# Attention, a mixture of experts and a feed-forward block in one kernel: activations carried across pairs, conversions moved, operands awaited singly, the plain block first

## The chip, the cores and the metric

One core of a Trainium2 chip runs the whole program. The metric is device time in microseconds (us): three runs of the kernel before gave a median of 2175.69 us (2173.25 to 2175.99). Engines are named as in the profile: PE does matrix products (PEld its weight loads), DVE and POOL elementwise work, ACT activations and copies, SP issues DMAs.

## The reference

Everything is float32. `q`, `k`, `v` have shape (4, 8, 576, 64).

```
x = attention(q, k, v)            # heads 0-3: a local window of 32; heads 4-7: every 32nd position, causal
x = x.transpose(0, 2, 1, 3).reshape(2304, 512)
P = exp(x @ w_gate - max)         # 2304 x 8
8 times: P /= row sums; P /= column sums; P *= 2304 / 8
for e in range(8): out += P[:, e] * (relu(x @ w1[e]) @ w2[e])     # w1[e] 512 x 1024, w2[e] 1024 x 512
h = out @ w_in                    # w_in 512 x 2048, stored as float64
g = where(h > 0, h, exp(min(h, 0)) - 1)
return g @ w_out                  # w_out 2048 x 512, stored as float64
```

## The kernel before

**Numbers.** PE multiplies in the format fp32r. Every operand is held as a rounded high part and a low part that carries the rest (`splits`, `low`: a cast on ACT, then a subtraction on DVE or POOL), and each product is three matmuls: high by high, high by low, low by high.

**Tiles.** The 2304 tokens go in two phases: phase 0 does 1024, phase 1 does 1024 and a plain block of 256. A hidden dimension is worked in *pairs* of two blocks of 128 columns: pairs 0 to 31 are the eight experts (four each, "MoE"), pairs 32 to 39 the last feed-forward block ("MoE2"). `gemm1` is the first product of a pair for 1024 tokens in Strassen's way (Winograd's form): seven products of six matmuls (128x512) each instead of eight. Its operands are seven sums of the tokens, B11, B21, B22, T1 to T4, held in `xb`, and seven sums of the weights. Three PSUM banks s1, s2, s3 gather the products; DVE adds between them (`add`, L943), so that the second use of s2 (S3 by T3) has to wait until `u2 = s2 + a1` has read it. `act` starts the activation of a finished quarter: a generator `activate` whose steps (ACT, DVE, and for MoE2 ACT and DVE again) `advance` takes one at a time. At the end of `gemm1` all are drained (L988). `gemm1_plain` is the ordinary first product for the 256 tokens. `gemm2` is the second product: for pairs taken two at a time (a *group*), two halves of four token tiles, 96 matmuls in all, in four banks `ybank`, which `finish` adds into `acc`.

**Order.** The order of every engine's queue is written out by hand: an engine runs its instructions in the order in which the program emits them. The program emits PE's matmuls and calls `gap` after every three of them in a first product (L938) and every three in a second product (L1030). `gap` puts one step each of side work into the queues: `prep_step` (the split of the next weights), `build_step` (the making of `xb` for the next layer: `build_a`, `build_b`, `build_plain`), `gate_step` (the gate's logits), and the generators in `gens`, each at its rate: the rest of the attention, `sinkhorn` (eight rounds of row and column sums), and `weigh` followed by `conversions` (float64 weights to float32, 32 jobs of seven DVE instructions and a store; the tile `val` has one buffer, so the next job begins when the store has landed). A generator's fourth entry says whether it runs in second products only: true for `sinkhorn` (rate 0.4), false for the conversions (rate 0.54). Builds run in second products only.

`ready(key)` emits all that is left of a named build: before a first product `a` (B11, B21), before its second product all of `b`. In phase 1 a group runs gemm1, plain, gemm1, plain, second product, plain second product.

The lines that matter are these:

```
if banks or alone_now[0] is None:          # gap, L755: builds
    for _ in range(BUILD_RATE): build_step()
...
ready((ph, moe2, "b"))                     # gemm1, L962
s2 = bank(); whole(prod(s2, S2, T2))
u2 = tmp("u2"); add(u2, s2, a1)
...
while acts: advance(acts)                  # gemm1, L988
```

Of the kernel before, what the change touches and what calls it, by code (L numbers as in the profile page):

```python
# [23 lines left out]
P = 128  # L24
# [16 lines left out]
HT = HALF // P  # L41
PW = 256
# [28 lines left out]
def sparse_attention_moe_kernel(ctx: ExitStack, tc: tile.TileContext, a, out):  # L71
# [159 lines left out]
    def build_a(src):  # L231

        hi, lo = xb
        todo = [(hi[:, x, c], lo[:, x, c], src(c + c0), ve if c else po_) for x, c0 in ((B11, 0), (B21, 2)) for c in (0, 1)]
        yield from splits(todo)

    def build_b(a, b):

        hi, lo = xb

        def minus(x, y, out=None):
            if out is None:
                out = hp_.tile([P, HALF], F32, tag="hh" if len(made) % 2 else "hl", name="t")
                made.append(out)
            ve.tensor_tensor(out=out, in0=x, in1=y, op=ALU.subtract)  # L245
            return out

        made = []
        t1 = [minus(b(c), a(c)) for c in (0, 1)]
        yield True  # L250
        t2 = [minus(b(c + 2), t1[c]) for c in (0, 1)]
        yield True

        def both(x, t, engs):
            for c in (0, 1):
                se.copy(hi[:, x, c], t[c])  # L256
            yield True
            for c in (0, 1):
                low(hi[:, x, c], lo[:, x, c], t[c], engs[c])
            yield True  # L260
# [236 lines left out]
    def att_s4(u):  # L497
# [144 lines left out]
    def build_step():  # L642
        if builds and next(builds[0][1], 0) == 0:
            builds.pop(0)

    def ready(key):
        while any(x[0] == key for x in builds):
            build_step()

# [84 lines left out]
    def after_attention():  # L734
# [5 lines left out]
        late["xp"] = [ffn.tile([P, 3, 2, PW], F32R, name=f"xp{hl}") for hl in "hl"]  # L740
        late["g"] = ctx.enter_context(tc.tile_pool(name="g", bufs=3))
        late["h"] = ctx.enter_context(tc.tile_pool(name="hplain", bufs=4))
# [3 lines left out]
        late["sink"] = sinkhorn()  # L746
        gens.append([late["sink"], SINK_RATE, 0.0, True])

    gens = []

    def gap(banks):
# [24 lines left out]
    def sinkhorn():  # L776
# [3 lines left out]
        yield True  # L780
        p1 = bank()
# [3 lines left out]
        p2 = bank()  # L785
        pe.matmul(p2[:, 0:1], ones[:1, :], small[:1, 1:2], start=True, stop=True)
# [7 lines left out]
        for it in range(8):  # L794
# [5 lines left out]
            yield True  # L800
            pc = bank()
            pe.matmul(pc[:, :E], ones, part, start=True, stop=True)
# [119 lines left out]

    def gemm1(ph, p, early=None):


        n = prep_state["now"] = ph * PAIRS + p
        w = slot_of(n, "done1")[:2]
        moe2 = p >= MOE1_PAIRS
        last = len(PHASES[ph]) == 1
        acts, hs = [], {}  # L930

        def prod(dst, wi, xi, start=True):
            for c in products(dst, w, xb, wi, xi, start=start):
                if c == 1 and last:
                    used(n, 1)
                yield c

        def whole(gen):  # L938
            for _ in gen:
                gap(False)  # L940

# [9 lines left out]

        ready((ph, moe2, "a"))
        s1 = bank()
        whole(prod(s1, A11, B11))
        a1 = tmp("a1")
        se.copy(a1, s1)  # L956
        if early:
            early()
            whole(prod(s1, A12, B21, start=False))
            act(s1, 0, 0)  # L960
# [8 lines left out]
        whole(prod(s3, S1, T1))  # L969
        advance(acts)  # L970
        whole(prod(s2, S3, T3, start=False))
        u3, c22 = tmp("u3"), tmp("c22")
        add(u3, s2, a1)
        add(c22, s3, u3)
        act(c22, 1, 1)
        advance(acts)
        if not early:
            whole(prod(s1, A12, B21, start=False))
            act(s1, 0, 0)
            advance(acts)  # L980
        whole(prod(s2, A22, T4, start=False))
        add(s2, s2, a1)
        act(s2, 1, 0)
        advance(acts)
        whole(prod(s3, S4, B22, start=False))
        add(s3, s3, u2)
        act(s3, 0, 1)
        while acts:  # L988
            advance(acts)
        return hs  # L990

    def gemm1_plain(ph, p):
        n = ph * PAIRS + p
        w = slot_of(n, "done1")[:2]
        ready((ph, p >= MOE1_PAIRS, "plain"))
        hs, acts = [], []
        for w1, w2, x2 in ((A11, A12, 1), (S1, A22, 2)):
            m = bank()
            for wi, xi in ((w1, 0), (w2, x2)):
                for _ in products(m[:, :PW], w, late["xp"], wi, xi, start=xi == 0, stop=xi != 0):  # L1000
                    gap(False)
            g = late["g"].tile([P, HALF], F32, tag="g", name="g")[:, :PW] if p >= MOE1_PAIRS else None
            hs.append([late["h"].tile([P, PW], F32R, tag=t, name=t) for t in ("ph", "pl")] + [g])
            acts.append(activate(p, m[:, :PW], PW, hs[-1]))
            advance(acts)
        while acts:
            advance(acts)
        used(n, 7)
        return hs

    def gemm2(ph, pairs, parts, tiles, t0):


        n0 = ph * PAIRS
        base = PHASES[ph][0][0]
        sums = [ybank() for _ in range(tiles)] if len(pairs) > 1 else [None] * tiles
        for p, hs in zip(pairs, parts):
            _, _, w2h, w2l = slot_of(n0 + p, "done")
            first, last = p == pairs[0], p == pairs[-1]
            for tt in range(tiles):  # L1020
                y = sums[tt] = sums[tt] or ybank()
                cs = slice(tt * P, (tt + 1) * P)
                for f in range(2):
# [6 lines left out]
                    gap(True)  # L1030

# [49 lines left out]

    def x1_a(ph):
        late["xa"] = r = raw("rawa")
# [6 lines left out]

    def x1_b(ph):
        r = late["xa"]
# [3 lines left out]

    def x1_plain(ph):
        r = late["p"].tile([P, KD, PW], F32, tag="rawp", name="rawp")
        for c in range(KD):
            pt = transposed(ybank(), 2 * HT, PW // P, c)  # L1100
            yield True
# [29 lines left out]
    def whole2(ph, pairs, hs):  # L1131
        for half in range(2):
            gemm2(ph, pairs, [by_half(x, half) for x in hs], HT, PHASES[ph][0][0] + half * HALF)
            if pairs[-1] == MOE1_PAIRS - 1:
                start_build((ph, True, "ab"[half]), (x1_a, x1_b)[half](ph))
        if len(PHASES[ph]) == 1:
            free_w2(len(pairs))


    h_prev = None  # L1140
    for p in range(SOLO):
        h_now = gemm1(0, p, early=(lambda: None) if p == 0 else None)
        if p:
            whole2(0, [p - 1], [h_prev])
        h_prev = h_now
    finish_gen(rest)


    for ph, blocks in enumerate(PHASES):
        for p in range(0 if ph else SOLO, PAIRS, GROUP):  # L1150
# [6 lines left out]
            for x in pairs:  # L1157
                hs.append(gemm1(ph, x, early=(lambda: None) if x == MOE1_PAIRS else None))
                if h_prev:
                    whole2(0, [SOLO - 1], [h_prev])  # L1160
                    h_prev = None
                if len(blocks) > 1:
                    hp.append(gemm1_plain(ph, x))
            if ph == 0 and p == PAIRS - GROUP:
                x_loads()
                start_build((1, False, "a"), build_a(lambda c: late["xa"][:, c]))
                start_build((1, False, "b"), x_b())
                start_build((1, False, "plain"), x_plain())
            whole2(ph, pairs, hs)
            if len(blocks) > 1:  # L1170
                gemm2(ph, pairs, hp, PW // P, blocks[1][0])
                free_w2(GROUP)
                if pairs[-1] == MOE1_PAIRS - 1:
                    start_build((ph, True, "plain"), x1_plain(ph))
            if ph == 0 and pairs[-1] == 2 * PER_E - 1:
                late["weigh"] = weigh()
                gens.append([late["weigh"], CONV_RATE, 0.0, False])

# [6 lines left out]
GATE_WAIT = 2  # L1185
GATE_WAIT1 = 2
RE_AT, RE_IN = 2, (4, 6)
# [3 lines left out]
X_DELAY = 4  # L1191
SINK_RATE = 0.4
CONV_RATE = 0.54

# [21 lines left out]
```

## Time and profile before

| | |
|---|---|
| median of three runs | 2175.69 us |
| the profiled execution | 2175.51 us |
| its span, first to last instruction | 2173.7 us, 26993 instructions |
| mean granted PE clock | 0.976 of full speed |
| busy share of the span | PE 95%, PEld 78%, DVE 61%, ACT 34%, POOL 29% |
| the chain that ended last | PE 62%, DVE 5%, ACT 3% |

A matmul's shown duration (0.39 us) is longer than the distance to the next one, because they are pipelined; so a busy PE need not be at its peak, and a stretch is better judged by how many matmuls it holds. "Idle" stands ahead of the arrow to what ended it. The chain and the waits name the last releaser only.

### The profile page before, as it was taken

What the parts mean: (1) busy time and instruction counts of PE and PEld (TensorE: products, weight loads), DVE (VectorE), ACT (ScalarE), POOL (GpSimd) and SP (SyncE); (2) the same over time, 40 slices, a digit from 0 to 9 for tenths busy, and PEclk for the clock granted to TensorE, in tenths of its full rate; (3) what the DMA queues carried; (4) which work ended last, traced back from release to release, by engine and by line L of the source; (5) the groups of instructions that cost most, each with busy time, mean ns of one, the idle gap of its engine ahead of it and who ended that gap; (6) DMA issues with size and microseconds to landing.
All of it is one profiled execution on the core that took longest, in us unless ns stands there. A gap on an engine that the chain in (4) does not pass through costs nothing.

```text
span 2173.7 us, 26993 instructions
## 1 busy us (share of the span) xinstructions
PE 2062.8 (95%) x10196; PEld 1697.5 (78%) x10196; DVE 1331.7 (61%) x2163; ACT 746.1 (34%) x1705; POOL 626.7 (29%) x709
## 2 busy tenths in 40 slices
PE   9889899999988999899999999999999999988999
PEld 7767677777766888677778888888888888867887
DVE  5676756888777855666664444444554445555555
ACT  6655322222222223355432222222222222234443
POOL 2332322333222333333342222222222222222220
PEclk8889999999999999899999999999999999999999
DMA  9632112333333311111321111111111111110111
GB/s 180 131 86 61 56 39 78 99 119 117 117 120 99 97 39 58 39 49 42 105 68 40 39 39 39 39 49 40 40 48 39 39 43 45 39 29 21 40 31 56
DMA packets 141171, 138.94 MB, mean 64 GB/s; under 512 B 67168, under 2 KB 105968, under 8 KB 141040
## 3 DMA queue, kind: packets, MB, share of 16 engines
q1 hardware_dynamic: 140080, 137.00, 21.7%
q8 instruction: 80, 1.31, 0.3%
q14 instruction: 51, 0.42, 0.1%
q10 hardware_dynamic: 960, 0.21, 0.1%
HBM read 121.46 MB, written 18.09 MB: 64 GB/s over the span
## 4 chain that ended last, share of the span: by engine, by line
PE 62%; DVE 5%; ACT 3%; DMA 1%; issue 1%; POOL 0%; SPq 0%; DVEq 0%; ACTq 0%
PE ybank L1026 34%; PE bank L881 28%; ACT g L904 1%; ACT g L903 1%; DVE xl L153 1%; DVE u L943 1%; DMA w_conv<-val 1%; DVE t L245 1%; ACT hh L908 1%; DVE g L906 0%; DMA w2raw<-in_moe_w 0%; DVE bank L943 0%; DVE c L943 0%; DVE acc L1040 0%; ACT xh L256 0%
## 5 line engine op out<-in xcount | busy, mean ns | idle before, releaser
L881 PE MATMUL bank<-xh,w1h 128*128 128x512 f32 x1120 | 454.9, 406 | 71.3 <-DVE u L943 42.8
L1026 PE MATMUL ybank<-w2h,hh 128*128 128x512 f32 x1280 | 505.5, 395 | 6.1 <-DVE kT L421 2.2
L1026 PE MATMUL ybank<-w2h,hl 128*128 128x512 f32 x1280 | 499.9, 391 | 0.0
L1026 PE MATMUL ybank<-w2l,hh 128*128 128x512 f32 x1280 | 499.8, 390 | 0.0
L881 PE MATMUL bank<-xl,w1h 128*128 128x512 f32 x1120 | 445.3, 398 | 0.2 <-DVE xl L153 0.2
L881 PE MATMUL bank<-xh,w1l 128*128 128x512 f32 x1120 | 443.8, 396 | 0.0
L1054 DVE SCALAR_TENSOR_TENSOR acc<-ybank,prob,acc 128x512 f32<-128x512 f32 x246 | 183.6, 748 | 297.4 <-PE ybank L1026 297.2
L143 ACT CAST w2h<-w2raw 128x512 fp32r<-128x512 f32 x160 | 94.9, 620 | 688.9 <-issue 455.7
L881 PEld LDWEIGHTS bank<-xh,w1h 128*128 128x128 f32 x1120 | 215.3, 192 | 136.0 <-DVE u L943 41.4
L153 POOL TENSOR_TENSOR w1l<-w1raw,w1h 128x256 fp32r<-128x256 f32 x240 | 196.9, 837 | 348.7 <-ACT w1h L143 345.8
L153 POOL TENSOR_TENSOR w2l<-w2raw,w2h 128x512 fp32r<-128x512 f32 x80 | 104.4, 1305 | 649.2 <-ACT w2h L143 642.3
L1026 PEld LDWEIGHTS ybank<-w2h,hh 128*128 128x128 f32 x1280 | 241.4, 189 | 57.2 <-DVE acc L1040 3.2
L1026 PEld LDWEIGHTS ybank<-w2h,hl 128*128 128x128 f32 x1280 | 241.1, 188 | 51.0
L1026 PEld LDWEIGHTS ybank<-w2l,hh 128*128 128x128 f32 x1280 | 241.5, 189 | 47.3
L881 PEld LDWEIGHTS bank<-xh,w1l 128*128 128x128 f32 x1120 | 215.2, 192 | 46.6
L881 PEld LDWEIGHTS bank<-xl,w1h 128*128 128x128 f32 x1120 | 215.6, 193 | 41.6 <-DVE xl L153 1.0
L943 DVE TENSOR_TENSOR u<-bank,a 128x512 f32<-128x512 f32 x160 | 110.3, 689 | 178.5 <-PE bank L881 116.9
L171 POOL TENSOR_TENSOR wsum<-w1raw 128x256 f32<-128x256 f32 x160 | 127.1, 794 | 295.2 <-DMA w1raw<-in_moe_w 202.9
L896 ACT ACTIVATE hh<-bank 128x512 fp32r<-128x512 f32 x192 | 113.9, 593 | 154.9 <-DVE bank L943 154.4
L153 DVE TENSOR_TENSOR w1l<-wsum,w1h 128x512 fp32r<-128x512 f32 (+1 forms) x164 | 129.6, 791 | 16.7 <-ACT w1h L143 16.7
L898 DVE SCALAR_TENSOR_TENSOR hl<-bank,hh 128x512 fp32r<-128x512 f32 x192 | 131.0, 682 | 7.9 <-ACT hh L896 1.5
L956 ACT COPY a<-bank 128x512 f32<-128x512 f32 x80 | 47.0, 587 | 171.3 <-PE bank L881 171.3
(178 smaller groups left out, 2727.8 us busy)
## 6 DMA issues: line engine op xcount, KB each, us to landing
w1raw<-in_moe_w SPq DMA_DIRECT2D x64, 512.0 KB, 3.4
w2raw<-in_moe_w SPq DMA_DIRECT2D x64, 512.0 KB, 3.5
raw<-in_moe_w_in SPq DMA_DIRECT2D x16, 512.0 KB, 4.0
w_conv<-val SPq DMA_DIRECT2D x32, 256.0 KB, 2.4
raw<-in_moe_w_out SPq DMA_DIRECT2D x16, 512.0 KB
w1raw<-w_conv SPq DMA_DIRECT2D x16, 512.0 KB, 3.5
w2raw<-w_conv SPq DMA_DIRECT2D x16, 512.0 KB, 3.6
q_t<-in_q SPq DMA_DIRECT2D x32, 144.0 KB, 3.8
```

The source lines that it names most:

```text
L143: se.copy(hi, src)
L153: eng.tensor_tensor(out=lo, in0=src, in1=hi.bitcast(F32), op=ALU.subtract)
L171: po_.tensor_tensor(out=o, in0=x, in1=y, op=op)
L245: ve.tensor_tensor(out=out, in0=x, in1=y, op=ALU.subtract)
L881: pe.matmul(dst, a_[:, wi, c, :], b_[:, xi, c, :], start=start and i == 0, stop=stop and i == 5, skip_group_check=True,)
L896: se.activation(hh, src, AF.Relu)
L898: ve.scalar_tensor_tensor(out=hl, in0=src, scalar=0.0, in1=hh.bitcast(F32), op0=ALU.max, op1=ALU.subtract)
L903: se.activation(g, src, AF.Relu, scale=-1.0)
L943: ve.tensor_tensor(out=out, in0=x, in1=y, op=ALU.add)
L956: se.copy(a1, s1)
L1026: pe.matmul(y, x[:, cs], w[:, f], start=first and f + m == 0, stop=last and f == 1 and m == 2)
L1054: ve.scalar_tensor_tensor(out=at, in0=y, scalar=prob[:, g, e : e + 1], in1=at, op0=ALU.mult, op1=ALU.add)
```

## The change

- **Activations.** `acts` becomes one list for the whole kernel. `gemm1` no longer drains it; `step()` (an `advance` and a `gap`) follows each product and its additions, the last ones run in the next pair, and `gemm2` drains them (`flush`) when it begins.
- **Side work.** `gap` is called once inside a product and once after it. Builds run in every gap. Up to two gate steps are taken per gap. Conversions run in second products only, at rate 0.85 (0.54 before); `sinkhorn` in all gaps, at 0.16 (0.4 before), in banks of `ybank` during first products.
- **Operands.** `build_a` and `build_b` note each finished operand in `built`, and `need(x)` emits build steps only until that operand is there. The gate's block waits likewise (and six steps more), and the attention's part that opens a new `xlate` tile first empties the gates' queue down to one.
- **Plain block.** In phase 1 a group runs plain, gemm1, plain, gemm1, plain second product, second product. Its `xp` is built ahead of `a` and `b`; its four products call `gap` once each.
- Buffers: `g` gets four instead of three; the program's DMA scratch goes from 1024 to 256.

```diff
@@ build_a
-        todo = [(hi[:, x, c], lo[:, x, c], src(c + c0), ve if c else po_) for x, c0 in ((B11, 0), (B21, 2)) for c in (0, 1)]
-        yield from splits(todo)
+        for x, c0 in ((B11, 0), (B21, 2)):
+            yield from splits([(hi[:, x, c], lo[:, x, c], src(c + c0), ve if c else po_) for c in (0, 1)])
+            built.add(x)
+            yield True
@@ att_s4
         if b > 1 and hf == 0:
+            while len(gates) > 1:
+                build_step()
+                gate_step()
             xs[b][hp] = at_p.tile([P, S], F32, tag="xlate", name="xlate")
@@ gate_block
-        for _ in range(GATE_WAIT1):
-            yield True
...
-            while any(x[0] == (0, False, "ab"[half]) for x in builds):
+            while not all(x in built for x, _ in parts):
+                yield True
+            for _ in range(GATE_WAIT1):
                 yield True
@@
+    def need(x):
+        while x not in built:
+            assert builds
             build_step()
@@ gap
-        if banks or alone_now[0] is None:
-            for _ in range(BUILD_RATE):
-                build_step()
-        gate_step()
+        for _ in range(BUILD_RATE):
+            build_step()
+        for _ in gates[:2]:
+            gate_step()
         for g in list(gens):
-            if g[3] and not banks:
+            if g[3] and not second[0]:
                 continue
@@ gemm1
+        def step():
+            advance(acts)
+            gap()
...
+        need(B11)
         s1 = bank()
-        whole(prod(s1, A11, B11))
+        prod(s1, A11, B11)
         a1 = tmp("a1")
         se.copy(a1, s1)
+        step()
...
-        ready((ph, moe2, "b"))
+        need(T2)
         s2 = bank()
-        whole(prod(s2, S2, T2))
+        prod(s2, S2, T2)
         u2 = tmp("u2")
         add(u2, s2, a1)
-        advance(acts)
+        step()
...
-        while acts:
-            advance(acts)
+        step()
         return hs
@@ groups of two pairs
-                hs.append(gemm1(ph, x, early=(lambda: None) if x == MOE1_PAIRS else None))
+                if len(blocks) > 1:
+                    hp.append(gemm1_plain(ph, x))
+                hs.append(gemm1(ph, x, early=x == MOE1_PAIRS))
...
+                start_build((1, False, "plain"), x_plain())
                 start_build((1, False, "a"), build_a(lambda c: late["xa"][:, c]))
                 start_build((1, False, "b"), x_b())
-                start_build((1, False, "plain"), x_plain())
-            whole2(ph, pairs, hs)
             if len(blocks) > 1:
                 gemm2(ph, pairs, hp, PW // P, blocks[1][0])
...
+            whole2(ph, pairs, hs)
+            free_w2(len(pairs))
@@ rates
-GATE_WAIT1 = 2
+GATE_WAIT1 = 6
-SINK_RATE = 0.4
-CONV_RATE = 0.54
+SINK_RATE = 0.16
+CONV_RATE = 0.85
```

## Rows read from the trace of the kernel before

**Rows 1.** The page's busy time and share by engine.

```profile
PE 2062.8 (95%) x10196; PEld 1697.5 (78%) x10196; DVE 1331.7 (61%) x2163; ACT 746.1 (34%) x1705; POOL 626.7 (29%) x709
```

**Rows 2.** Windows: length, busy PE PEld DVE ACT POOL (instructions), PEclk, DMA.

```profile
231.00:295.00 64.00, 53.55 (x221) 41.77 (x221) 52.39 (x123) 18.05 (x36) 17.92 (x22) 0.92 0.16 50
300.00:350.00 50.00, 49.79 (x220) 40.72 (x219) 20.06 (x28) 16.28 (x32) 16.25 (x20) 1.00 0.16 53
350.00:740.00 390.00, 355.40 (x1505) 283.44 (x1504) 321.61 (x504) 97.47 (x196) 119.08 (x129) 0.98 0.34 110
750.00:900.00 150.00, 150.00 (x671) 123.98 (x669) 83.18 (x118) 44.49 (x89) 52.71 (x62) 1.00 0.16 48
898.70:935.60 36.90, 27.34 (x102) 20.50 (x101) 26.92 (x39) 19.32 (x36) 9.23 (x8) 0.81 0.14 43
935.60:1067.00 131.40, 124.46 (x539) 101.57 (x538) 80.35 (x121) 63.24 (x121) 43.92 (x50) 0.99 0.18 56
1067.00:1112.00 45.00, 38.46 (x171) 30.96 (x170) 40.79 (x51) 22.13 (x43) 24.13 (x20) 0.96 0.35 119
1150.00:1900.00 750.00, 750.00 (x3635) 634.71 (x3634) 369.51 (x553) 198.89 (x409) 197.84 (x230) 1.00 0.14 42
1935.60:1962.80 27.20, 14.84 (x53) 10.66 (x52) 21.60 (x31) 14.29 (x26) 7.03 (x6) 0.79 0.13 39
1962.80:2165.00 202.20, 198.33 (x945) 166.21 (x945) 111.72 (x180) 87.47 (x181) 40.26 (x45) 0.99 0.11 35
```

**Rows 3.** Waits of PE, whole span: total us, times, longest us.

```profile
PE bank L881 <- DVE u L943: 42.8, 25, 5.3
PE bank L881 <- DVE hl L898: 20.3, 12, 4.1
PE bank L802 <- DVE small L799: 10.2, 5, 6.3
PE bank L881 <- ACT xh L256: 4.6, 2, 3.0
```

**Rows 4.** Groups of DVE, 350 to 740 us: busy us, mean ns, idle before.

```profile
L1054 DVE SCALAR_TENSOR_TENSOR acc<-ybank,prob,acc 128x512 f32<-128x512 f32 x64 | 47.1, 743 | 7.0 <-PE ybank L1026 6.8
L817 DVE SCALAR_TENSOR_TENSOR val<-raw,val 128x512 f32<-128x512 uint32 x32 | 28.2, 881 | 0.6
L831 DVE SCALAR_TENSOR_TENSOR val<-val,expo 128x512 f32<-128x512 f32 x32 | 26.4, 827 | 0.2
L827 DVE SCALAR_TENSOR_TENSOR expo<-raw,expo 128x512 int32<-128x512 int32 x32 | 25.0, 780 | 0.3
L943 DVE TENSOR_TENSOR u<-bank,a 128x512 f32<-128x512 f32 x34 | 23.4, 687 | 10.9 <-PE bank L881 10.7
L815 DVE TENSOR_SCALAR val<-raw 128x512 int32<-128x512 int32 x32 | 17.0, 532 | 34.0 <-DMA w_conv<-val 25.4 <-issue 7.9 <-DMA raw<-in_moe_w_in 0.5
L821 DVE TENSOR_SCALAR expo<-raw 128x512 int32<-128x512 int32 x32 | 16.4, 512 | 0.0
L823 DVE TENSOR_SCALAR expo<-expo 128x512 int32<-128x512 int32 x32 | 16.2, 505 | 0.7
L825 DVE TENSOR_SCALAR expo<-expo 128x512 int32<-128x512 int32 x32 | 15.1, 472 | 0.6
```

**Rows 5.** DVE in order of time in a second product: start us, us.

```profile
443.05 1.26 DVE L831 SCALAR_TENSOR_TENSOR val<-val,expo 128x512 f32<-128x512 f32 x1
444.24 0.74 DVE L1054 SCALAR_TENSOR_TENSOR acc<-ybank,prob,acc 128x512 f32<-128x512 f32 x1
446.81 0.43 DVE L815 TENSOR_SCALAR val<-raw 128x512 int32<-128x512 int32 x1 [1.83 <-issue]
```

**Rows 6.** Groups of DVE, 230 to 300 us.

```profile
L806 DVE TENSOR_TENSOR prob<-prob,small 128x144 f32<-128x144 f32 x8 | 3.4, 430 | 0.3
L797 DVE RECIPROCAL small<-small 128x18 f32<-128x18 f32 x8 | 2.1, 266 | 0.3
```

**Rows 7.** Window just after a wait of PE that lasted 4.1 us.

```profile
702.00:706.00 4.00, 4.00 (x13) 2.91 (x12) 3.83 (x8) 2.72 (x6) 2.20 (x3) 0.57 0.00 0
```

More of the change, by code (lines that the diff above doesn't have):

```diff
@@ L259, in both @@
                 low(hi[:, x, c], lo[:, x, c], t[c], engs[c])
+            built.add(x)
             yield True
@@ L740, in after_attention @@
         late["xp"] = [ffn.tile([P, 3, 2, PW], F32R, name=f"xp{hl}") for hl in "hl"]
-        late["g"] = ctx.enter_context(tc.tile_pool(name="g", bufs=3))
+        late["g"] = ctx.enter_context(tc.tile_pool(name="g", bufs=4))
         late["h"] = ctx.enter_context(tc.tile_pool(name="hplain", bufs=4))
@@ L746, in after_attention, with spare_bank, gap @@
         late["sink"] = sinkhorn()
-        gens.append([late["sink"], SINK_RATE, 0.0, True])
+        gens.append([late["sink"], SINK_RATE, 0.0, False])
     gens = []
-    def gap(banks):
+    second = [False]
+    def spare_bank():
+        return bank() if second[0] else ybank()
+    def gap():
         for _ in range(PREP_FAST if prep_state["now"] < SOLO + PER_E else PREP_RATE):
             prep_step()
-        if banks or alone_now[0] is None:
-            for _ in range(BUILD_RATE):
-                build_step()
-        gate_step()
+        for _ in range(BUILD_RATE):
+            build_step()
+        for _ in gates[:2]:
+            gate_step()
         for g in list(gens):
-            if g[3] and not banks:
+            if g[3] and not second[0]:
                 continue
@@ L780, in sinkhorn @@
         yield True
-        p1 = bank()
+        p1 = spare_bank()
         pe.transpose(p1[:1, :P], mx, ident)
@@ L784, in sinkhorn @@
         yield True
-        p2 = bank()
+        p2 = spare_bank()
         pe.matmul(p2[:, 0:1], ones[:1, :], small[:1, 1:2], start=True, stop=True)
@@ L800, in sinkhorn @@
             yield True
-            pc = bank()
+            pc = spare_bank()
             pe.matmul(pc[:, :E], ones, part, start=True, stop=True)
@@ L921, in used, with gemm1 @@
             prep_state["used"] = 0
-    def gemm1(ph, p, early=None):
+    acts = []
+    def gemm1(ph, p, early=False):
         n = prep_state["now"] = ph * PAIRS + p
         w = slot_of(n, "done1")[:2]
-        moe2 = p >= MOE1_PAIRS
-        last = len(PHASES[ph]) == 1
-        acts, hs = [], {}
+        hs = {}
         def prod(dst, wi, xi, start=True):
+            need(xi)
             for c in products(dst, w, xb, wi, xi, start=start):
[L934 to L940, printed above, removed]
+                if c == 0:
+                    gap()
+            used(n, 1)
         def add(out, x, y):
@@ L950, in tmp, with c11 @@
             return up_.tile([P, HALF], F32, tag="u", name=name)
-        ready((ph, moe2, "a"))
+        def step():
+            advance(acts)
+            gap()
+        def c11():
+            prod(s1, A12, B21, start=False)
+            act(s1, 0, 0)
+            step()
+        need(B11)
         s1 = bank()
-        whole(prod(s1, A11, B11))
+        prod(s1, A11, B11)
         a1 = tmp("a1")
         se.copy(a1, s1)
+        step()
         if early:
-            early()
-            whole(prod(s1, A12, B21, start=False))
-            act(s1, 0, 0)
-            advance(acts)
-        ready((ph, moe2, "b"))
+            c11()
+        need(T2)
         s2 = bank()
-        whole(prod(s2, S2, T2))
+        prod(s2, S2, T2)
         u2 = tmp("u2")
         add(u2, s2, a1)
-        advance(acts)
+        step()
+        need(T1)
         s3 = bank()
-        whole(prod(s3, S1, T1))
-        advance(acts)
-        whole(prod(s2, S3, T3, start=False))
+        prod(s3, S1, T1)
+        step()
+        prod(s2, S3, T3, start=False)
         u3, c22 = tmp("u3"), tmp("c22")
@@ L975, in gemm1, with flush @@
         act(c22, 1, 1)
-        advance(acts)
+        step()
         if not early:
[L978 to L981, printed above, removed]
+            c11()
+        prod(s2, A22, T4, start=False)
         add(s2, s2, a1)
         act(s2, 1, 0)
-        advance(acts)
-        whole(prod(s3, S4, B22, start=False))
+        step()
+        prod(s3, S4, B22, start=False)
         add(s3, s3, u2)
         act(s3, 0, 1)
+        step()
+        return hs
+    def flush():
         while acts:
             advance(acts)
-        return hs
     def gemm1_plain(ph, p):
@@ L995, in gemm1_plain @@
         ready((ph, p >= MOE1_PAIRS, "plain"))
-        hs, acts = [], []
+        hs = []
         for w1, w2, x2 in ((A11, A12, 1), (S1, A22, 2)):
@@ L1000, in gemm1_plain @@
                 for _ in products(m[:, :PW], w, late["xp"], wi, xi, start=xi == 0, stop=xi != 0):
-                    gap(False)
+                    pass
+                gap()
             g = late["g"].tile([P, HALF], F32, tag="g", name="g")[:, :PW] if p >= MOE1_PAIRS else None
@@ L1005, in gemm1_plain @@
             advance(acts)
-        while acts:
-            advance(acts)
-        used(n, 7)
         return hs
@@ L1015, in gemm2 @@
         base = PHASES[ph][0][0]
+        flush()
+        second[0] = True
         sums = [ybank() for _ in range(tiles)] if len(pairs) > 1 else [None] * tiles
@@ L1029, in gemm2 @@
                         finish(ph, p, g, g - base // P, y)
-                    gap(True)
+                    gap()
+        second[0] = False
     def finish(ph, p, g, tile_, y):
@@ L1080, in transposed, with x1_a @@
         return pt
-    def x1_a(ph):
+    def x1_a():
         late["xa"] = r = raw("rawa")
@@ L1089, in x1_a, with x1_b @@
         yield from build_a(lambda c: r[:, c])
-    def x1_b(ph):
+    def x1_b():
         r = late["xa"]
@@ L1134, in whole2 @@
             if pairs[-1] == MOE1_PAIRS - 1:
-                start_build((ph, True, "ab"[half]), (x1_a, x1_b)[half](ph))
-        if len(PHASES[ph]) == 1:
-            free_w2(len(pairs))
+                if half == 0:
+                    built.clear()
+                start_build((ph, True, "ab"[half]), (x1_a, x1_b)[half]())
     h_prev = None
     for p in range(SOLO):
-        h_now = gemm1(0, p, early=(lambda: None) if p == 0 else None)
+        h_now = gemm1(0, p, early=p == 0)
         if p:
             whole2(0, [p - 1], [h_prev])
+            free_w2(1)
         h_prev = h_now
@@ L1157, in sparse_attention_moe_kernel @@
             for x in pairs:
-                hs.append(gemm1(ph, x, early=(lambda: None) if x == MOE1_PAIRS else None))
+                if len(blocks) > 1:
+                    hp.append(gemm1_plain(ph, x))
+                hs.append(gemm1(ph, x, early=x == MOE1_PAIRS))
                 if h_prev:
                     whole2(0, [SOLO - 1], [h_prev])
+                    free_w2(1)
                     h_prev = None
-                if len(blocks) > 1:
-                    hp.append(gemm1_plain(ph, x))
             if ph == 0 and p == PAIRS - GROUP:
                 x_loads()
+                built.clear()
+                start_build((1, False, "plain"), x_plain())
                 start_build((1, False, "a"), build_a(lambda c: late["xa"][:, c]))
                 start_build((1, False, "b"), x_b())
-                start_build((1, False, "plain"), x_plain())
-            whole2(ph, pairs, hs)
             if len(blocks) > 1:
                 gemm2(ph, pairs, hp, PW // P, blocks[1][0])
-                free_w2(GROUP)
                 if pairs[-1] == MOE1_PAIRS - 1:
-                    start_build((ph, True, "plain"), x1_plain(ph))
+                    start_build((ph, True, "plain"), x1_plain())
+            whole2(ph, pairs, hs)
+            free_w2(len(pairs))
             if ph == 0 and pairs[-1] == 2 * PER_E - 1:
                 late["weigh"] = weigh()
-                gens.append([late["weigh"], CONV_RATE, 0.0, False])
+                gens.append([late["weigh"], CONV_RATE, 0.0, True])
 WARM0, WARM1, WARM_MOD, WARM_OF, WARM_N = 14, 10, 2, 1, 512
```

7 lines of the change are left out of this document (4 added, 3 removed).

## The prediction

> **What bounds the kernel now.** I read the page's busy times first: PE is busy 2062.8 of 2173.7 us [rows 1]. So 111 us of idle time, and what PE loses at a low clock, is all that a change of order can give back; the products themselves stay the same in number and shape. Next the windows by stage, which say where the loss sits [rows 2]. In an undisturbed stretch (300 to 350 us) 220 matmuls of 512 columns take 50 us: 0.227 us each. By that pace the stages lose:
> - 350 to 740 us, the conversions: 390 - 1505 x 0.227 = 48 us.
> - 231 to 295 us, the row and column sums: 10.5 us idle (64 - 53.55) and, at a mean clock of 0.92, some 5 us of half speed (64 x 0.08): 15.5 us.
> - 898.7 to 935.6 us, the first two first products of MoE2 in phase 0: 84 matmuls (19.1 us) and the transposes between them (some 2 us) leave 16 us.
> - 935.6 to 1067 us, the rest of MoE2 in phase 0: 131.4 - 539 x 0.227 = 9 us.
> - 1067 to 1112 us, the passage to phase 1: 147 matmuls of 512 columns and 24 of 256 (at about 0.12) are 36.3 us, so 8.7 us.
> - 1935.6 to 1962.8 us, MoE2 in phase 1, the first pair up to the plain block: 42 matmuls and 8 transposes are 10.4 us, so 16.8 us.
> - 1962.8 to 2165 us, the rest of it: the mixed pace of 1150 to 1900 us is 750/3635 = 0.206, so 202.2 - 945 x 0.206 = 7 us.
>
> Together 121 us. From 750 to 900 and from 1150 to 1900 us PE is busy without a break: there is nothing to gain there. Last the waits: PE stands for DVE's `u` additions (42.8 us) and `hl` (20.3 us), both in first products, and for the sums of `sinkhorn` (10.2 us) [rows 3]. PE is the engine on the path and DVE, late in its queue, is what stops it.
>
> **The change part by part.**
>
> *Conversions (48 us now).* The seven rows of DVE sum to 144.3 us for 32 jobs, 4.5 us a job; 34 us more DVE stood idle ahead of the job's first instruction, L815, 1.06 us a job [rows 4]. A group of two pairs is 180 matmuls, 40.8 us of PE. Its DVE work without conversions is 83.18 us in 150, or 22.6 us in 40.8 [rows 2]. Now a group has 60 gaps at 0.54, 32.4 steps; a job is 8 steps, so 4.05 jobs: 22.6 + 4.05 x (4.5 + 1.06) = 45.1 us. DVE is full, and the group takes as long as DVE: 4.3 us over PE's 40.8, near the loss shown (48 us over 8.2 groups, 5.9 each; 8 steps of `weigh` and 256 of jobs are 264, over 32.4).
>
> After, a group has 32 gaps at 0.85, 27.2 steps, 3.4 jobs, and the stage lasts 264/27.2 = 9.7 groups. The jobs come faster inside a second product, so less lies between a job's last instruction, L831, and the next L815, which cannot begin until the store has landed. The row shows 444.31 to 446.81, 2.5 us, of which one `finish` fills 0.74 [rows 5]. With two gaps and a third between them, half of which bring a `finish`, I take 1.6 us of idle time a job (from 1.06, the mean now, to 2.5 where nothing lies between). DVE in a group: 22.6 + 3.4 x (4.5 + 1.6) = 43.3 us. That is a floor of 2.5 us over PE, 24 us for the stage, if the excess is spread. It isn't: a second product is 96 matmuls, 21.8 us, and DVE has in it 8 additions of 0.743 us (5.9), 3.4 jobs (20.7 with their waits), two splits of weights (1.4) and the last two `hl` that `flush` emits (1.4): 29.4 us, 7.6 late. These 7.6 us stand ahead of the next pair's `u2`. That has to be done after three products (4.1 us), when PE comes back to bank s2; it takes 0.69 us itself. PE waits 7.6 + 0.7 - 4.1 = 4.2 us a group, 41 us in all: a gain of 7 us. The ends are 48 (all of it hidden) and -25 (1.2 us more for a job's idle time, or a lower clock, below).
>
> *Row and column sums (15.5 us).* 13 steps, each a round of nine small DVE operations of 0.27 to 0.43 us [rows 6], about 3 us; PE's matmul opens the next step. At 0.4 the steps are 2.5 gaps (1.7 us) apart, so PE comes too early. At 0.16 they are 6.25 gaps (4.2 us) apart, over 81 gaps, 55 us. That covers the chain; but DVE has 52.4 us of work in this stretch [rows 2], and now part of it falls in first products. Without its loss the stretch is 48.5 us, so at least 4 us stay. Ends: gain 0 to 11.5; I take 7.
>
> *Activations carried over.* In MoE2 the four steps of three activations are drained at the end of a pair, and the next `u2` stands behind them: one wait of 2.5 us a group. Spread over the next pair's steps they lie under its first two products (2.7 us). 9 us becomes 3 (gain 6; ends 2 to 8); in phase 1 7 us becomes 2 (gain 5; ends 2 to 6). In the experts' part without conversions there is no wait to remove: 0. The fourth buffer of `g` covers the activations that are open at once.
>
> *Operands awaited singly.* At the start of MoE2 in phase 0 all of `b`, some 15 DVE operations (12 us), stands ahead of `u2`. With `need`, T2 comes as late as before, `u2` follows it, then T1, T3, T4, B22 one product ahead of their use. But DVE's 12 us have to be done inside this pair all the same (9.5 us, with 6 us of its own additions and activations), so only the overlap is won: 16 becomes 12 (ends 0 to 8).
>
> *Plain block first.* In phase 1 `xp` is now made during the second product, 15 steps in the first half's 16 gaps, so its wait (about 5.5 of the 16.8 us) goes. The 24 matmuls of 256 columns, 2.9 us, lie under the start of `b`. What is late next is T2 and T3, as in phase 0. 16.8 becomes 9 (gain 7.5; ends 3 to 12). At the passage to phase 1 the plain block and the first product (4.3 us) cover `b`'s first half: 8.7 becomes 3 (gain 6; ends 0 to 8). For the sixteen groups of experts in phase 1 the new order costs nothing as long as PE's cover holds: DVE has 370 us of work in 750, and each bank's last reader is emitted at least a plain product (1.5 us) before its next use. If that cover were gone, 0.7 us a pair would come up, 22 us.
>
> *The attention's added loop.* It empties the gates' queue when batch 2 opens its first `xlate`, inside the first pair. The gate's second half needs T1 and B22, so all of `b` and two blocks of gate matmuls go into the queues there, and PE, in order, waits for B22. Queued behind that wait on PE are the rest of this pair and the attention's next products, which ACT and DVE wait for. Today PE loses about 4.6 us to these casts and does only twelve of its own matmuls (2.7 us) meanwhile [rows 3]. I take 4 us lost (ends 0 and 10). Gates taken two at a time, the later release of weight slots and the smaller scratch move work on engines that are not full: nothing.
>
> **Sum.** 7 + 7 + 6 + 5 + 4 + 7.5 + 6 - 4 = 38.5 us. From the profiled execution's 2175.5 us (0.2 under the median of the runs): 2137 us.
>
> **The rivals.**
> - *The bursts are harmless.* If DVE's excess spreads and the group meets its floor of 2.5 us or less, the conversions lose 15 to 24 us, not 41, and the time is 2137 - 22 = 2115, down to 2100 with the other terms at their better ends. For it: second products now show almost no wait of PE. Against it: DVE is full already. Chance 0.25.
> - *The conversions cost more than now.* One mechanism: 3.4 jobs crowd into 21.8 us, the stores are waited for in full (2.5 us a job, 3 us more a group), and each group has one long wait of PE after which the clock falls. After a wait of 4.1 us the granted clock was 0.57 for the next 4 us, 13 matmuls where 17.6 fit, about 1 us [rows 7]. That makes 4.2 + 3 + 1 = 8.2 us a group, 80 us for the stage: 32 us more than now. With the other terms at 60% (19 us) the time is 2175.5 + 32 - 19 = 2188. It decides once a group's loss passes 48 + 31, over 9.7: 8.1 us. The Trainium skill (TensorE: Matmul & The Clock Gate, HAM oscillation) tells of a kernel in which a wait in every tile kept bringing the engine back to the low clock; this trace agrees for single waits over 4 us and shows no such series. Chance 0.12.
> - *The waits only move.* DVE has as much to do as before, and what the activations gain the conversions and the added loop take: 2171 to 2180. Against it: 45 us of the loss lie outside the conversions, in waits of known cause. Chance 0.1.
>
> **How the numbers follow.** Forecast 0.53, with its own range 2118 to 2158; the rivals 0.25, 0.12 and 0.10. Of a measurement of this kernel 0.2% (4.4 us) can be told from no change. Faster: 0.53 + 0.25 + a part of the third, 0.82; within 0.2%: 0.06; slower: 0.12. For 8 in 10 I reach to 2100 below, the better ends of the first rival, and to 2178 above, short of the second.
>
> **What would show it.** Conversions: waits of PE for `u` once a group, at a group's first pair, of some 4 us, and none in second pairs; second products with DVE full. If L1026 waits for `acc` by several us a group, or the window just after a group's wait shows a clock near 0.5, the second rival is right. Sums: L802's wait below 5 us. MoE2: no wait of 2.5 us before a second pair's S3 by T3; in phase 1 no wait for `xph`. Attention: one wait of PE of about 10 us for B22 near 100 us. The forecast is wrong if the stage of the conversions loses under 25 or over 60 us.

## The result and the profile after

The changed kernel takes 2194.61 us (median of four runs, 2192.7 to 2200.29) against 2174.47 for the kernel before on the same chip: a ratio of 1.010, with a 95% interval of 1.0076 to 1.0125. It is slower by 20 us, where 38 us less were forecast. The profiled executions differ by as much (spans of 2193.2 and 2173.7 us), so the trace can say where.

Windows of the changed kernel, with the columns of [rows 2]. The edges are the starts of PE's first matmul of a stage: the sums, the conversions (pairs 6 to 29), the group of pairs 30 and 31, the start of MoE2 in phase 0, the rest of it, the start of phase 1, its experts, the start of MoE2 there, and the rest up to the last second product.

```profile
243.50:307.90 64.40, 56.46 (x245) 45.19 (x244) 45.03 (x108) 17.68 (x35) 18.51 (x22) 0.97 0.15 50
307.90:877.60 569.70, 516.12 (x2162) 407.65 (x2161) 403.25 (x623) 142.45 (x290) 171.26 (x193) 0.98 0.28 89
877.60:922.30 44.70, 43.34 (x197) 35.16 (x196) 24.32 (x35) 15.04 (x30) 15.89 (x18) 1.00 0.14 47
922.30:980.10 57.80, 48.20 (x198) 36.35 (x197) 39.45 (x56) 26.64 (x50) 18.41 (x19) 0.94 0.11 37
980.10:1114.30 134.20, 126.27 (x541) 100.31 (x540) 90.80 (x129) 67.39 (x130) 48.63 (x51) 1.00 0.24 77
1114.30:1177.00 62.70, 54.28 (x253) 45.07 (x252) 33.86 (x49) 17.63 (x36) 19.92 (x21) 0.95 0.15 47
1177.00:1960.80 783.80, 783.75 (x3805) 662.83 (x3804) 385.34 (x577) 208.12 (x431) 209.77 (x244) 1.00 0.13 41
1960.80:2029.20 68.40, 60.10 (x270) 47.35 (x269) 43.13 (x66) 30.87 (x62) 19.00 (x19) 0.93 0.10 32
2029.20:2162.00 132.80, 130.32 (x637) 109.04 (x636) 80.29 (x129) 65.56 (x137) 27.55 (x29) 1.00 0.11 32
```

Cut at the same matmuls, every kernel of this study gives a column (us, one profiled execution each, from pair 0's first matmul on; names as in the experiments; conv_old, thin, val2 and the rest without the a_ or b_ ahead of them, gv_thin for a_gap_val_thin):

```
stage                  before  after  conv_old conv_new thin  val2 gapfirst flush ready pl_last gap_in gap_val gv_thin b_val2
to the sums (pair 4)    154.8  152.8   152.2   156.5  152.4  152.2  151.7  152.9  152.3  152.4  152.8  154.8  154.1  156.6
sums                     68.5   64.4    64.4    68.4   64.2   64.6   65.4   66.6   64.3   64.1   63.2   65.6   63.6   67.9
conversions (6 to 29)   539.6  569.7   550.3   567.8  543.7  521.1  568.8  570.8  570.3  571.4  567.5  508.6  511.6  515.7
pairs 30, 31             42.7   44.8    44.6    42.8   44.7   44.6   44.8   44.7   44.7   44.7   42.8   42.8   42.7   42.8
MoE2 phase 0, start      58.7   57.7    59.2    58.9   59.1   58.8   58.8   58.2   58.0   59.1   54.9   54.8   54.9   57.3
MoE2 phase 0, rest      134.8  134.3   134.2   135.4  134.3  133.9  134.4  137.1  134.6  136.8  128.6  128.7  128.6  134.9
phase 1, start           58.4   62.7    61.2    58.3   62.7   62.7   64.3   62.6   62.5   59.6   66.5   65.9   64.8   58.4
phase 1, experts        785.1  783.8   783.8   785.0   783.8   783.8   787.5   783.8   784.0  813.0  787.8  787.6  787.3  785.1
MoE2 phase 1, start      72.3   68.4    69.1    72.2   68.5   68.4   66.5   68.4   68.3   68.7   65.2   64.7   65.0   72.1
MoE2 phase 1, rest      134.6  132.9   132.8   134.6  132.9  132.8  132.9  133.3  132.9  137.5  133.5  133.7  133.3  134.6
```

One row carries the result: the conversions' stage is 30 us longer. All the other rows together, and a start that is 2.5 us earlier, give 10.5 us back. Twelve groups at PE's pace (180 matmuls of 0.227 us each) are 490 us, so the stage loses 80 us, not 50. Its first and last group have no conversions yet or no more; the ten between them (350.7 to 834.7 us) take 484 us, 76 over PE's pace.

PE's waits (total, times, longest) while the conversions run, from 371 to 880 us of the changed kernel, then from 357 to 753 us of the kernel before (`hl` is the low part of an activation):

```profile
PE bank L901 <- DVE u L960: 25.4, 9, 3.7
PE ybank L1052 <- DVE acc L1081: 15.6, 18, 2.9
PE bank L901 <- DVE hl L918: 8.7, 6, 1.6
```

```profile
PE bank L881 <- DVE hl L898: 20.0, 11, 4.1
PE bank L881 <- DVE u L943: 13.3, 12, 2.1
PE ybank L1026 <- DVE acc L1054: 0.9, 1, 0.9
```

Second products, which had no wait to speak of, now wait for `acc` 18 times; the waits for `u` are fewer but longer. How one comes about is seen in DVE's own order (start, length, idle before) where the second product of pairs 10 and 11 ends, at 447.3 us, and pair 12 begins:

```profile
446.24 0.69 DVE L851 SCALAR_TENSOR_TENSOR val<-val,expo 128x512 f32<-128x512 f32 x1
446.85 0.74 DVE L1081 SCALAR_TENSOR_TENSOR acc<-ybank,prob,acc 128x512 f32<-128x512 f32 x1
449.53 0.43 DVE L835 TENSOR_SCALAR val<-raw 128x512 int32<-128x512 int32 x1 [1.93 <-DMA w_conv<-val]
449.99 0.69 DVE L837 SCALAR_TENSOR_TENSOR val<-raw,val 128x512 f32<-128x512 uint32 x1
450.60 0.75 DVE L1081 SCALAR_TENSOR_TENSOR acc<-ybank,prob,acc 128x512 f32<-128x512 f32 x1
451.26 0.42 DVE L841 TENSOR_SCALAR expo<-raw 128x512 int32<-128x512 int32 x1
451.60 0.75 DVE L1081 SCALAR_TENSOR_TENSOR acc<-ybank,prob,acc 128x512 f32<-128x512 f32 x1
...
454.31 0.68 DVE L960 TENSOR_TENSOR u<-bank,a 128x512 f32<-128x512 f32 x1
```

Three of the second product's additions (L1081) and most of a job still stand in DVE's queue when PE has gone on to the next pair. PE needs `u` at 451.5 and gets it after 454.3. Ahead of that, from 447.6 us on, DVE itself had stood idle for 1.93 us, for the store. Windows of the same place, columns as above:

```profile
447.30:451.50 4.20, 4.20 (x19) 3.19 (x17) 2.23 (x5) 1.11 (x2) 0.00 (x0) 1.00 0.58 189
451.50:455.00 3.50, 0.04 (x1) 0.00 (x0) 3.47 (x8) 0.00 (x0) 0.00 (x0) 0.87 0.00 0
455.00:461.00 6.00, 5.95 (x14) 4.69 (x15) 2.50 (x4) 1.69 (x4) 0.99 (x1) 0.51 0.36 91
461.00:473.00 12.00, 12.00 (x54) 9.91 (x54) 9.69 (x15) 5.72 (x12) 4.23 (x6) 1.00 0.29 87
```

PE is stopped for 3.5 us, and then the granted clock is at 1.2 GHz (0.51) for 6 us, in which 14 matmuls start where 26 would fit: another 2.7 us, as an estimate (12 x 0.227). "Busy" shows none of that (5.95 of 6).

### The profile page after: what moved, and what is told of

Its sections match the earlier page's. It is cut to its first block, busy times and chain, and to the rows that moved or that the text cites. A ratio compares the mean times of both kernels' runs of the same rounds, so it can differ in the third digit from the quotient of the medians.

```text
span 2193.2 us, 26962 instructions
## 1 busy us (share of the span) xinstructions
PE 2068.4 (94%) x10196; PEld 1688.2 (77%) x10196; DVE 1325.6 (60%) x2163; ACT 740.2 (34%) x1705; POOL 624.5 (28%) x709
## 4 chain that ended last, share of the span: by engine, by line
PE 54%; DVE 4%; ACT 3%; DMA 2%; issue 1%; POOL 0%; SPq 0%; DVEq 0%; ACTq 0%
PE ybank L1052 30%; PE bank L901 23%; DMA w2raw<-in_moe_w 1%; ACT g L924 1%; DVE xl L153 1%; ACT g L923 1%; ACT hh L928 1%; DVE t L247 1%; DVE u L960 0%; DMA w2raw<-w_conv 0%; DVE w2l L153 0%; DMA rawp<-x_late 0%; ACT w1h L143 0%; ACT w2h L143 0%; DVE w1l L153 0%
## 5 line engine op out<-in xcount | busy, mean ns | idle before, releaser
L1052 PE MATMUL ybank<-w2h,hh 128*128 128x512 f32 x1280 | 507.6, 397 | 17.5 <-DVE acc L1081 15.6
L1081 DVE SCALAR_TENSOR_TENSOR acc<-ybank,prob,acc 128x512 f32<-128x512 f32 x246 | 183.9, 749 | 267.2 <-PE ybank L1052 266.9
L153 DVE TENSOR_TENSOR w1l<-wsum,w1h 128x512 fp32r<-128x512 f32 (+1 forms) x164 | 116.5, 712 | 2.6 <-ACT w1h L143 2.6
L916 ACT ACTIVATE hh<-c 128x512 fp32r<-128x512 f32 x64 | 40.4, 632 | 182.5 <-DVE c L960 182.5
```

The costliest lines, as they stand in the source:

```text
L153: eng.tensor_tensor(out=lo, in0=src, in1=hi.bitcast(F32), op=ALU.subtract)
L916: se.activation(hh, src, AF.Relu)
L1052: pe.matmul(y, x[:, cs], w[:, f], start=first and f + m == 0, stop=last and f == 1 and m == 2)
L1081: ve.scalar_tensor_tensor(out=at, in0=y, scalar=prob[:, g, e : e + 1], in1=at, op0=ALU.mult, op1=ALU.add)
```

## The experiments

**Which part costs: the conversions put back, and moved alone.** Theory A: crowding the conversions into second products. Theory B: the new place of the gap in a first product.

```diff
 a_conv_old (from the changed kernel)
-  gens.append([late["weigh"], CONV_RATE, 0.0, True])     CONV_RATE = 0.85
+  gens.append([late["weigh"], CONV_RATE, 0.0, False])    CONV_RATE = 0.54
 b_conv_new (from the kernel before): the reverse
```

> The changed kernel, with the conversions alone put back: in all gaps, at rate 0.54. Theory A (crowding the conversions into the second products is what costs): their stage loses 48 us again instead of some 79, so 31 us less than the changed kernel: 2163 us (2155 to 2172), faster than before by the rest of the change. Theory B (the new place of the gap in the first product costs in every group, the conversions are innocent): 2188 to 2198 us, as the changed kernel.

> The kernel before, with the conversions alone changed: in second products only, at rate 0.85. Theory A: 31 us more than before: 2205 us (2195 to 2215), with one wait of PE for u of 3 to 4 us in every group of the stage. Theory B: 2170 to 2180 us.

Measured: a_conv_old 2175.39 us, ratio to before 1.0011 (0.9991 to 1.0031); b_conv_new 2201.76 us, ratio 1.0135 (1.0109 to 1.0161). The move alone costs 29 us on the old kernel and 19 on the new one: it is the main cause, and b_conv_new lies in A's range. a_conv_old does not: with the move undone the rest of the change gains nothing either, where A expected 11 us. Its stage still takes 550.3 us, 10.7 more than before. Something in the first products costs too. PE's waits tell the two apart. Those of b_conv_new (354 to 840 us), which has the old place of the gap:

```profile
PE bank L881 <- DVE u L943: 31.3, 9, 4.7
PE ybank L1026 <- DVE acc L1054: 17.0, 22, 3.0
PE bank L881 <- DVE hl L898: 0.8, 2, 0.4
```

The waits for `u` and `acc` come with the move; the changed kernel's 8.7 us for `hl` do not.

**Is it DVE's sum, or a wait inside its queue?**

```diff
 a_conv_thin: in all gaps, CONV_RATE = 0.42
 a_val2, b_val2:
-  ... tag="val", name="val", bufs=1)
+  ... tag="val", name="val", bufs=2)
```

> The changed kernel with the conversions in all gaps at rate 0.42, so that they reach over all eleven groups that are there. Theory A in its form 'DVE is full': a group has 3.15 jobs, 22.6 + 3.15 x 5.56 = 40.1 us of DVE against 40.8 of PE, so most of the stage's loss goes: 2136 us (2125 to 2150). If it is not DVE's sum but each single placement that costs, as many waits of 1 to 2 us a group stay: 2160 to 2175. Theory B: 2185 or more.

> The changed kernel with two buffers for val, so that a job need not wait for the store of the one before. Theory A with the store's wait as the main term: DVE loses 63 us of idle time in the stage, has 37.9 us a group and 22.7 in a second product of 21.8, so the waits for u and for acc nearly go: 2135 us (2125 to 2155). Theory A with the bare work of the jobs as the main term: a third of it, 2175 (2165 to 2185). Theory B: 2188 to 2198.

> The kernel before with two buffers for val and nothing else. If the store's wait is a main term there too (34 us of idle DVE, in a stage that DVE fills): 15 to 30 us less than before, 2145 to 2160. Rival (in the kernel before the conversions' placing among the additions costs, not the wait): 2168 to 2176.

Measured: a_conv_thin 2168.43 us, ratio 0.9982 (0.9965 to 0.9998); a_val2 2145.35, ratio 0.9881 (0.9854 to 0.9908); b_val2 2149.54, ratio 0.9894 (0.9867 to 0.9922). Thinning the conversions until DVE's work per group fits under PE's gave 26 us of the 58 expected from DVE's sum, as the rival named there said (2160 to 2175): DVE is busy 313.0 of the 402.4 us of nine such groups, and PE still waits 28.6 us for `hl` and 5.7 for `u`. The sum is not what decides. The second buffer, which changes no amount of work, gave 49 us, and 24 on the kernel before; both times lie in the ranges expected for the store's wait. DVE's first instruction of a job, in the stage (busy us, mean ns, idle before), in the changed kernel and in a_val2:

```profile
L835 DVE TENSOR_SCALAR val<-raw 128x512 int32<-128x512 int32 x32 | 15.4, 482 | 63.1 <-DMA w_conv<-val 51.6 <-issue 10.4 <-DMA raw<-in_moe_w_in 1.1
```

```profile
L835 DVE TENSOR_SCALAR val<-raw 128x512 int32<-128x512 int32 x32 | 20.2, 632 | 2.1 <-DMA raw<-in_moe_w_out 1.2 <-DMA raw<-in_moe_w_in 1.0
```

61 us of idle DVE went, and PE's waits for `u` in the stage with them:

```profile
PE bank L901 <- DVE hl L918: 13.7, 10, 1.5
PE ybank L1052 <- DVE acc L1081: 4.3, 2, 3.0
PE bank L901 <- DVE u L960: 0.2, 1, 0.2
```

**What eats the rest: the late w2.** In a_val2 mainly one kind of wait is left, for `hl`, once a group, and the group without conversions (pairs 30, 31) still takes 44.6 us, against 42.7 before. Theory W: ACT is held up by a cast that waits for the load of the next w2, and holds up the activations behind it.

```diff
 a_gapfirst (only after the first product of a pair)
         a1 = tmp("a1")
+        gap()
         se.copy(a1, s1)
-        step()
+        advance(acts)
```

> The changed kernel; only after the first product of a pair the order is turned: the gap's side work first, then the copy of a1 and the advance (as in the kernel before). Theory W (the second cast of w2 now stands behind the copy of a1 on ACT, so the next weights are loaded some 2.6 us later, and ACT, waiting for them, holds up the activations): the group without conversions (44.8 us from pair 30 to MoE2) comes back to 42.7, MoE2 of phase 0 (134.3 us from pair 34 to phase 1) falls to about 129, the conversions lose up to 10 us less; 2174 us (2165 to 2185). Rival (the missing gains lie in the carried activations themselves): 2188 to 2198 and the stages as in the changed kernel.

Measured: 2200.96 us, ratio 1.0128 (1.0105 to 1.0151), the stages within 4 us of the changed kernel's. The expectation failed, because the edit did not move the load: it is issued 4.4 us after a group's start, against 4.3 in the changed kernel and 1.7 in the kernel before (the groups of pairs 30 and 31). What still stood behind was DVE's half of the split, w2l, emitted one gap after the addition that follows the second of the seven products, and so behind `u2`. So the whole placing was undone:

```diff
 a_gap_in
             for c in products(dst, w, xb, wi, xi, start=start):
-                if c == 0:
-                    gap()
+                gap()
...
         def step():
             advance(acts)
-            gap()
```

> The changed kernel with both gaps of a product inside it again, ahead of its additions (step only advances the activations). Theory W, mended (it is the split w2l, now queued behind u2 on DVE, that delays the load of the next w2 by some 2.7 us; turning the copy of a1 could not help): the group without conversions falls from 44.8 to at most 42.7 us, MoE2 of phase 0 from 134.3 to about 129, the conversions' groups by 1 to 2 us each; 2175 us (2165 to 2185). Rival (the waits for hl and g come from something else): stages and total as in the changed kernel, 2188 to 2200.

Measured: 2183.81 us, ratio 1.0057 (1.0036 to 1.0078). The load is issued 1.6 us after the start of the group without conversions, which falls to 42.8 us, and MoE2 of phase 0 to 128.6, as expected; the conversions' stage falls only from 569.7 to 567.5, and the passage to phase 1 and its experts lose 7.8 us, so the total is just inside the expected range, 9 us above its middle. PE's waits (370 to 872 us) show why the stage gains so little:

```profile
PE bank L901 <- DVE u L959: 32.4, 9, 4.3
PE ybank L1050 <- DVE acc L1079: 15.3, 18, 2.5
```

The waits for `hl` are gone, but those for `u` have risen from 25.4 to 32.4 us: what the gap gives back is lost again at `u`. ACT in order of time at the start of a group of MoE2, in the kernel before, in the changed one and in a_gap_in:

```profile
1002.35 0.59 ACT L956 COPY a<-bank 128x512 f32<-128x512 f32 x1 [6.18 <-PE bank L881]
1006.05 1.14 ACT L143 CAST w2h<-w2raw 128x512 fp32r<-128x512 f32 x2 [3.11 <-DMA w2raw<-w_conv]
1007.88 0.63 ACT L903 ACTIVATE g<-c 128x512 f32<-128x512 f32 x1 [0.69 <-DVE c L943]
```

```profile
981.62 0.59 ACT L982 COPY a<-bank 128x512 f32<-128x512 f32 x1 [6.86 <-PE bank L901]
982.11 0.62 ACT L143 CAST w2h<-w2raw 128x512 fp32r<-128x512 f32 x1
988.03 1.14 ACT L143 CAST w2h<-w2raw 128x512 fp32r<-128x512 f32 x2 [5.30 <-DMA w2raw<-w_conv]
989.08 0.63 ACT L923 ACTIVATE g<-c 128x512 f32<-128x512 f32 x1
```

```profile
970.65 0.59 ACT L980 COPY a<-bank 128x512 f32<-128x512 f32 x1 [6.18 <-PE bank L901]
974.03 1.14 ACT L143 CAST w2h<-w2raw 128x512 fp32r<-128x512 f32 x2 [2.79 <-DMA w2raw<-w_conv]
976.18 0.63 ACT L923 ACTIVATE g<-c 128x512 f32<-128x512 f32 x1 [1.00 <-DVE c L959]
```

Read from the copy of `a`: the casts that wait for the load come 3.7 us later in the kernel before, 6.4 in the changed one, 3.4 in a_gap_in. In the outer two the activation `g` waits for DVE's `c`, as it should; in the middle one it starts the moment that ACT is done with the casts, late.

**The other parts undone, one at a time**, read from the stages, with a single run of each.

```diff
 a_flush: at the end of gemm1   + while acts: advance(acts)
 a_ready: gemm1   need(B11), need(T2)  ->  need(B21), need(B22)
 a_plain_last: phase 1 in the old order (gemm1, plain; second product, plain second product; builds a, b, plain; a pair's weights are released behind its plain block)
```

> The changed kernel with the activations drained at the end of each first product again. Theory W: the carrying over is worth something, but its gain is eaten by the late weights: MoE2 of phase 0 rises from 134.3 to some 139 us. Rival (carrying is worth nothing): 134.3 within 0.5.

> The changed kernel with whole builds awaited again (B21 where B11 was asked, B22 where T2 was). If awaiting singly is worth what the stages show at most: the start of MoE2 in phase 0 (57.7 us) rises by 1 to 3 us, in phase 1 (68.4 us) by 1 to 3; the total by 2 to 6 us. Rival (DVE's sum decides, the order does not): all stages within 0.5 us.

> The changed kernel with the plain block put last again in phase 1, and its operands built last. If plain first is the cause of the longer start of phase 1 (62.7 us against 58.4 before) and of the shorter start of MoE2 there (68.4 against 72.3): 58 to 59 and 71 to 73, total unchanged within 3 us. Rival (the longer start comes from builds in every gap or from the awaited operands): 62 to 63.

Measured: a_flush 2202.15 us; MoE2 of phase 0 rises by 2.8 us, the sums by 2.2, the conversions by 1.1: carrying is worth some 6 us here, as far as one execution shows; MoE2's 137.1 lies between the two expectations. a_ready 2194.54; the start of MoE2 moves by 0.3 and 0.1 us: awaiting singly is worth nothing beside the rest. a_plain_last 2230.62; the start of phase 1 does fall, to 59.6, but the start of MoE2 stays (68.7), and the experts of phase 1 rise by 29 us, which was not expected. There PE's wait is again `hl`:

```profile
PE bank L901 <- DVE hl L918: 20.2, 23, 1.4
```

And ACT (1178 to 1991 us) stands for the loads of w2, which it does not in the experts of phase 1 of the changed kernel:

```profile
ACT w2h L143 <- DMA w2raw<-in_moe_w: 78.3, 15, 5.4
```

So in phase 1 the plain block hides the late w2 that the moved gap makes: it pays there for another part of the same change. That is read from these waits; no run has the old order together with the old place of the gap in the changed kernel.

**Both mended.**

> The changed kernel with both gaps inside the product and two buffers for val. If the store's wait and the late w2 are two causes that add: 2145 - 20 = 2125 us (2112 to 2135). If they are one (either alone frees DVE enough): 2140 to 2150.

> As a_gap_val, with the conversions in all gaps at rate 0.42. If what is left of the conversions' loss is crowding into second products: some 10 us under a_gap_val. If conversions in first products delay u2 as they did in the kernel before: 5 to 15 us over it.

Measured: a_gap_val (gaps inside, two buffers for `val`) 2128.09 us, ratio 0.9792 (0.9769 to 0.9814): faster than the kernel before by 45 us and than the changed one by 67. The causes add, as expected (2112 to 2135). With `val` mended, the gap's place is worth 17 us, without it 11; that difference is within the noise of the totals, but the conversions' stage has it too (521.1 to 508.6 us, against 569.7 to 567.5). a_gap_val_thin 2130.06, ratio 0.9803 (0.978 to 0.9826): neither 10 us under a_gap_val nor 5 over it, as the two expectations had it. Once the store isn't waited for, it makes no difference clear of the noise where the conversions run. The conversions' stage of a_gap_val:

```profile
308.60:817.20 508.60, 500.17 (x2161) 404.35 (x2161) 413.37 (x623) 144.26 (x291) 175.31 (x193) 0.99 0.32 100
```

The same 623 DVE instructions as in the changed kernel's 569.7 us: 61 us less for the same work.

## Why the prediction was wrong, point by point

*What bounds the kernel* held: PE is the path, DVE late in its order stops it, and the losses lie in the stages named.

*Conversions: the step that failed.* "PE waits 7.6 + 0.7 - 4.1 = 4.2 us a group, 41 us in all: a gain of 7 us." The place was right: jobs and additions still queued ahead of `u2` at the first pair's third product. The sum was wrong, because it booked the whole loss as that one wait. The stage lost 80 us, 76 of them in the ten groups with conversions, 7.6 each; this step is 37 of the 58 us between forecast and result. The waits for `u` were smaller than forecast: 25.4 us, 2.5 a group. What the sum put at nothing made the difference: 15.6 us for `acc` inside second products and 8.7 for `hl`, which b_conv_new, with the old place of the gap, hardly has (0.8). All of PE's idle time in the stage is 53.6 us (569.70 - 516.12). The low clock is an estimated 11 us of the rest (a mean of 0.98 over 569.7 us); the other 15 are what remains. They fit with the way idle time is shown: a matmul is drawn with 0.39 us, so some 0.16 us of every longer distance between two starts does not show as idle. The idle time at a store was 63.1/32 = 1.97 us, not the 1.6 taken.

The second rival had this place and this price (80 us, 8.2 a group), with a chance of 0.12, and of its two signs one came, a clock near 0.5 after a group's wait, and the other in part: the waits for `acc` are 1.6 us a group, not several. That its number came out is in part luck: it had 7.2 us a group in one wait for `u`, where 2.5 were measured and `acc` and `hl` took 2.4, and the store was not waited for in full (1.97 us a job, not 2.5). Its 1 us a group for the clock was about right on average. The Trainium skill (TensorE: Matmul & The Clock Gate, HAM oscillation) tells of a kernel that a wait in every tile brought back to the low clock each time. The changed kernel's trace agrees with that in part: PE waits in each of the ten groups, and the mean granted clock is below full in five of them (0.93, 0.93, 0.97, 0.96 and 0.97; 1.00 in the others).

The reasoning behind the size was wrong as well: DVE's load per group was taken for what decides. a_conv_thin, which fits that sum, kept 54 us of loss in the stage; a_val2, with the sum of work unchanged, kept 31.

*A part that had no price.* That `gap` moved from before a product's additions to behind them was told in the change and costed nowhere. It puts w2l behind `u2`, the load of the next w2 2.7 us later, and ACT's casts in front of the activations. That is why the terms for MoE2 failed: activations carried over, 6 us forecast in phase 0, 0.5 measured; its start there, 4 and 1.0; the start in phase 1, 7.5 and 3.9; the rest of phase 1, 5 and 1.7. With the gaps inside, a_gap_in shows 6.2, 3.8, 7.1 and 1.1: the forecast's terms were there, but for the last.

*Operands awaited singly*: forecast to win overlap; a_ready shows nothing.

*Plain block first*: 6 us of gain forecast at the passage to phase 1, 4.3 lost. PE waits 6.4 us there for `pl`, the plain block's activation: it is queued on DVE behind the rest of `b`, and holds the bank that gemm1 wants next. The fall in the start of MoE2 that was put down to the new order stays when the order is undone (68.7 against 68.4). For the experts of phase 1 "the new order costs nothing as long as PE's cover holds" was right: 783.8 us against 785.1. The 22 us named for the loss of that cover were not tested; the 29 us of a_plain_last are another cost, that of the late w2.

*Sums*: 7 forecast, 4.1 measured; PE still waits 7.9 us for `small` there, where less than 5 was the sign named. *The attention's loop*: 4 lost forecast; the stage is 2 us shorter, and the wait of PE near 100 us is 4.3 us long (for `xh`), not 10. Why was not tried.

## What to carry to other kernels

A wait in the middle of an in-order queue costs whatever stands behind it: before work is moved to an engine's quieter stretch, look at what that work itself waits for, and give the buffer that it waits on a second copy first. When side work is moved past an instruction that waits, follow what its own next step triggers (here a split, a load, a cast) to the engine that will stand for it. A part can look worth much only because it hides another part's cost, so undo parts singly and read the stages, not the total.

## What was not expected of the hardware

After a stop of PE of 3.5 us (451.5 to 455.0) the granted clock was 0.51 for 6 us of closely packed matmuls, and that stretch cost nearly as much (2.7 us) as the stop. It is not so after every stop: after one of 3.2 us for the same `u` addition (columns as above) the clock stays full and all 26 matmuls fit.

```profile
790.10:793.30 3.20, 0.04 (x2) 0.02 (x1) 3.20 (x7) 0.00 (x0) 0.00 (x0) 1.00 0.03 13
793.30:799.30 6.00, 6.00 (x26) 4.97 (x27) 2.61 (x4) 1.88 (x4) 1.18 (x1) 1.00 0.23 87
```
